# Five reorderings in a forward and backward SSM-convolution / SiLU block on one core

## The chip, the core and the metric

The kernel runs on one of the eight cores of one Trainium2 chip. A core has five engines that run side by side, each with an instruction queue of its own that it works through strictly in order, and they wait for each other through semaphores. TensorE (PE) multiplies matrices into PSUM, VectorE (DVE) and ScalarE (ACT) do element-wise work and copy PSUM to SBUF, GpSimd (POOL) does small element-wise work and issues DMAs, SyncE (SP) only issues DMAs. PSUM here is eight banks of 128 partitions x 2 KB. The metric is the device time of one execution in microseconds (us).

## The reference

Four residual layers run on a [2048, 448] activation, and then the gradient of all of it is taken:

```python
x = A_q
x = x + A(layernorm(x), k, v, shift_k, ssm_k, ssm_D)   # layer 0: long convolution, gated
x = x + B(layernorm(x), w1, w2)                        # layer 1: silu(x w1) w2
x = x + A(layernorm(x), k, v, shift_k, ssm_k, ssm_D)   # layer 2
x = x + B(layernorm(x), w1, w2)                        # layer 3

A: kv = (four-tap causal shift of k with shift_k) * v
   y  = irfft(rfft(kv, 4096) * rfft(ssm_k, 4096))[:2048] + kv * ssm_D
   return q * y
```

It returns x and the gradients of A_q, A_k, A_v, shift_k, ssm_k, ssm_D, w1 and w2 for a given grad_out. k, v and the filter are the same in layers 0 and 2, so y is computed once. All data is bf16, sums are float32.

## The kernel before

Rows are laid out so that partition p holds rows 16p to 16p + 15; a chunk c is four of these 16 row tiles. The kernel has three stages.

**Prefix** (`_ssm_prefix`, to about 102 us) computes y (`Ysb`) by FFTs written as matmuls. A first stage multiplies by `M1sb` (`_fft_stage1`, L206, and `stage1_kv`, L399, for kv), 128 x 128 blocks are turned on PE (`turn`, L361, seven groups of 16), and a second stage multiplies by `Gsb` (`_fft_stage2`, L217, in 14 chunks of 1024 columns, `NCI` = 14). ssm_k is transformed first. Then the shift convolution (`conv`, L383) runs over two halves h of the channels and four row groups; in the second half two of the 14 chunks of the filter's second stage (`Ka`) follow each conv, that is eight of them, and the other six follow the loop. `_swap_halves_dma` (L244, L245) makes from `Ka` a copy `KB` with the two partition halves exchanged, by two DMAs on POOL's queue for each pair of chunks. Also in this loop the layernorm of the first four row tiles runs step by step (`ln0`, `_ln_steps`: statistics on DVE, rstd by a power on POOL, L270, normalised rows `na0` on ACT, L276). After the loop kv is turned and gets its second stage; `cons_prod` copies each chunk (`A1K`), multiplies it on DVE with `Ka` and `KB` (`pab`, L467), and `_fft_inv_stage2_chunk` (L226, L227) does the first inverse stage into the PSUM tile `ps_v`, copied to `B1` (`A1kv`), two chunks later. At the end 16 turns of a part of grad_out (`ps_t`, copied to `gT0`, L485) and eight matmul groups (`ps_y`, L492) give `Ysb`, copied by DVE (the first) and ACT (the other seven). All PSUM tiles of the prefix rotate through four buffers of two banks (tag `A`).

**Main** (`Main.run`) goes over the four chunks c. `H` multiplies by w1 (`ps_h`, L509) and applies silu, `O` by w2 (`ps_o`, L691) and adds to the residual `X` (L695), `G` is the gradient through w2 (`ps_g`, L509; its result is copied on ACT, L719, or multiplied by the silu slope on DVE, L861), `N` the gradient through w1 and the layernorm (`ps_n`, L737). `T` turns four row tiles on PE (`ps_t`, L576) and copies them on ACT (L577). Letters in `weave` and `steps` say in which order steps of these generators are traced; PE's queue keeps this order, the other engines' queues are set by a scheduler that works from the traced order. `fwd0(c)` and `fwd0b(c)` are the first norm with the gate and the second norm of a chunk (L278 on DVE is the normalised result). `ps_o` and `ps_n` share two PSUM banks (tag `po`). `store` (L562, L566, L568) sends every activation tile through a DMA transpose on SP's queue and writes it to DRAM (`a_d`, `g_d`).

**Jobs and suffix.** The weight gradients are products over all 2048 rows. `Jobs` cuts them into blocks of four matmuls (`J` in the patterns; `ps_d`, L1023 in `opening`, L988 in `mms`) that are woven into the last chunk of `Main` and into `_ssm_suffix`, which computes the gradients of the convolution. A job reads one of the stored tiles again as its stationary side (`dstat`, 512 KB, loaded in `load`: the fourth to sixth on POOL's queue, L977, the others on SP's, L982) against one of four moving tensors of 1792 KB: grad_out (`go`), the gradient in `X`, and the normalised rows n3 (`n3m`, loaded by `load_n3`, L1083) and n1 (`n1m`, L1076). `n3m` takes the SBUF of `w2T`, `n1m` that of `go`.

`issue_after(i)` places an instruction behind instruction i in the same queue. It is an order and no wait for i's end.

Of the kernel before, what the change touches and what calls it, by code (L numbers as in the profile page):

```python
# [10 lines left out]
FP32 = mybir.dt.float32  # L11
# [6 lines left out]
P = 128  # L18
S = 2048
D = 448  # L20
F = 1792
J = 16
# [8 lines left out]
NCI = SPEC // 1024  # L31
# [186 lines left out]
        consume(ci, ps)  # L218


def _fft_inv_stage2_chunk(k, pa, pb, conj, B1, ci, psum, cnd=False):
    nc = k.nc
    ga, gb = (G_IAC, G_IBC) if conj else (G_IA, G_IB)
    pv = psum.tile([P, 8, P], FP32, name="ps_v", **k.pt["v"])
    for i in range(8):
        nc.tensor.matmul(pv[:, i, :], lhsT=pa[:, i * P:(i + 1) * P], rhs=k.Gsb[:, ga, :], start=True, stop=False)  # L226
        nc.tensor.matmul(pv[:, i, :], lhsT=pb[:, i * P:(i + 1) * P], rhs=k.Gsb[:, gb, :], start=False, stop=True)  # L227
    if cnd:
        _copy(nc, k.bal.pick(1024), B1[:, :, 32 * ci:32 * ci + 32].rearrange("p q (dh ds) -> p dh q ds", ds=4),
              pv[:].rearrange("p dh (q ds) -> p dh q ds", ds=4))  # L230
    else:
        _copy(nc, k.bal.pick(1024), B1[:, 8 * ci:8 * ci + 8, :].rearrange("p a b -> p (a b)"), pv[:].rearrange("p a b -> p (a b)"))
# [56 lines left out]
def _ssm_prefix(k):  # L289
    nc, tc = k.nc, k.tc  # L290
# [3 lines left out]
    with ExitStack() as es:  # L294
# [110 lines left out]
        def cons_ka(ci, ps):  # L405
            sl = slice(ci * 1024, (ci + 1) * 1024)
            _copy(nc, bal.pick(1024), Ka[:, sl], ps[:])
            if ci % 2 == 1:
                lo, hi = (ci - 1) * 1024, (ci + 1) * 1024
                if ci > 8:  # L410
                    _swap_halves_dma(k, KB, Ka, lo, hi, nc.gpsimd)

        k.gb0 = _hd(k, [P, 4, D], "gb0")
        with tc.issue_after(w2.ins):
# [5 lines left out]
        for h in range(2):  # L420
            for i, jq in enumerate((1, 2, 3, 0)):
                kvt = conv(h, jq)
                if prev:
                    stage1_kv(*prev)
                prev = (h, jq, kvt)
                if h == 0:
                    for g in (2 * i, 2 * i + 1):
                        if g < 7:
                            turn(A1Kf, Z, g)
                else:  # L430
                    _fft_stage2(k, Z, psum, cons_ka, range(2 * i, 2 * i + 2))
                    next(ln0, None)
        for _ in ln0:
            pass
        for i in range(4):
            _swap_halves_dma(k, KB, Ka, 2048 * i, 2048 * (i + 1), nc.gpsimd)
        stage1_kv(*prev)
        _fft_stage2(k, Z, psum, cons_ka, range(8, NCI))

        for i in range(7):  # L440
            nc.gpsimd.dma_start(out=k.SPEC_d["K"][:, 2048 * i:2048 * (i + 1)], in_=Ka[:, 2048 * i:2048 * (i + 1)])
# [34 lines left out]
        k.X = k.wk.tile([P, NT, D], BF16, name="X", tag="WX")  # L476
        k.gT0 = k.X[:].rearrange("p t d -> p (t d)")[:, 11 * D:11 * D + 2048].rearrange("p (b t) -> p b t", b=ND)
        for pa, pb, cj in hold:
            _fft_inv_stage2_chunk(k, pa, pb, False, B1, cj, psum)
        pt = psum.tile([P, ND, 512], BF16, name="ps_t", tag="A", bufs=4)  # L480
        for b, (lo, hi) in enumerate(BLK):
            for tl in range(4):
                nc.tensor.transpose(pt[:, b, tl * P:(tl + 1) * P], k.gb0[:, tl, lo:hi], k.ident[:])
        _copy(nc, bal.pick(2048, dve_ns=0.53), k.gT0, pt[:])

        B1v = B1.rearrange("p a (c n s) -> p a c n s", c=2, n=16)
        for i in range(8):
            py = psum.tile([P, 2, 512], FP32, name="ps_y", tag="A", bufs=4)
            for u in range(2):
                n2 = 2 * i + u  # L490
                for c in range(2):
                    nc.tensor.matmul(py[:, u, :D].rearrange("p (dh ds) -> p dh ds", ds=4), lhsT=k.Minvsb[:, n2, c, :], rhs=B1v[:, :, c, n2, :], start=(c == 0), stop=(c == 1))  # L492
            _copy(nc, nc.vector if i == 0 else nc.scalar, k.Ysb[:, 2 * i:2 * i + 2, :], py[:, :, :D])

# [37 lines left out]
class Main:  # L534
# [21 lines left out]
    def store(self, key, tile_, c, hh):  # L556
        nc, k = self.nc, self.k
        dst = k.OP_d[key]
        prev = None
        for lo, hi in ((0, 4), (4, 7)):  # L560
            an = self.t([P, 4, 4, P], "turned", "S", 2)
            i = nc.sync.dma_start_transpose(out=an[:, 0:hi - lo].rearrange("p a t f -> p (a t) f"), in_=tile_[:, lo:hi, :].rearrange("p a s -> p (a s)"))  # L562
            args = dict(out=dst[:, 7 * hh + lo:7 * hh + hi, 4 * c:4 * c + 4, :], in_=an[:, 0:hi - lo])
            if prev is not None:
                with self.tc.issue_after(i.ins):
                    nc.sync.dma_start(**prev)  # L566
            prev = args
        nc.sync.dma_start(**prev)  # L568

    def transp(self, src, dst, h):  # L570
        nc, k = self.nc, self.k
# [208 lines left out]
    def run(self, es):  # L780
# [52 lines left out]
        for c in range(4):  # L833

            aT2, dT2 = r
            self.slope(dT2)
            if c < 3:
                self.fwd0(c + 1)
            nT = self.nT() if c < 3 else None
            o = self.O(c, 1, aT2)  # L840
            steps("OOOO", O=o)
            if c < 3:
                self.fwd0b(c + 1)
            if c == 0:
                weave("O" * 4, O=o)
            else:
                if c == 1:
                    gh2, g = gh21, g21
                else:
                    gh2 = []  # L850
                    g = self.G(gT, gh2)
                if c == 1:
                    weave("OGGOGGOTOT", O=o, G=g, T=self.T(self.n0[c + 1][1], nT))
                elif c < 3:
                    weave("OGOGGOGGGGTOT", O=o, G=g, T=self.T(self.n0[c + 1][1], nT))
                else:
                    jobs.start()
                    weave("OGOGGOGGGGO", O=o, G=g)
            for lo, hi in ((0, 4), (4, 7), (7, 8), (8, 12), (12, 13), (13, 14)):
                g = gh2[lo // 7][:, lo % 7:lo % 7 + hi - lo, :]  # L860
                nc.vector.tensor_tensor(out=g, in0=self.dpart(dT2, lo, hi), in1=g, op=ALU.mult)  # L861
            if c < 3:
                for hh in range(2):
                    self.store(("g", 1), gh2[hh], c, hh)
            gbc = gb
            n = self.N(c, 1, gh2, lambda tl: gbc[:, tl, :], self.n1[1], self.n1[0])
            G2 = self.X[:, 4 * c:4 * c + 4, :]
            gT = self.nT()
            gh1, dT0 = [], dT1
            tg = self.T(G2, gT)  # L870
            if c < 3:
                r = []
                if c == 0:
                    weave("NTNTNHNNHHNNHHNHH", N=n, T=self.T(self.n0[1][1], nT), H=self.H(c + 1, 0, nT, r, (10, 11)))
                else:
                    weave("NHNNHHNNHHNNHHN", N=n, H=self.H(c + 1, 0, nT, r))
                gb = gb_load(c + 1)
                aT, dT1 = r
                weave("OOOOOOTOTO", O=self.O(c + 1, 0, aT), T=tg)
                self.fwd1(c + 1, [self.chain] * 4)  # L880
                g = self.G(gT, gh1, dT0)
                if c:
                    gT = self.nT()
                    self.load_gT(c + 1, gT)
                    weave("G" * 7, G=g)
                else:
                    weave("G" * 7, G=g)
                self.slope(dT1, self.last_copy)
            else:
                weave("NJNJNJNJNJNJNJN", N=n, J=jg)  # L890
                for hh in range(2):
                    self.store(("g", 1), gh2[hh], c, hh)
                weave("J" * 14 + "TJTJJ", T=tg, J=jg)
                weave("GGGJJGGJJGGJJ", G=self.G(gT, gh1, dT0, (1, 3, 5)), J=jg)
            for hh in range(2):
                self.store(("g", 0), gh1[hh], c, hh)
            n = self.N(c, 0, gh1, lambda tl: self.X[:, 4 * c + tl, :], self.n0[c][1], self.n0[c][0])
            if c < 3:
                r = []
                nT = self.nT()  # L900
                weave("NNTNTNHNNHHNNHHHH", N=n, T=self.T(self.n1[1], nT), H=self.H(c + 1, 1, nT, r, (10, 11)))
            else:
                weave("NJNNJNNJNNJN", N=n, J=jg)
# [14 lines left out]
class Jobs:  # L918
# [48 lines left out]
    def load(self, key, ft):  # L967
# [8 lines left out]
        if i in (3, 4, 5):  # L976
            nc.gpsimd.dma_start(out=st[:], in_=src[:, ft, :, :])  # L977
            return st
        with ExitStack() as es:
            if self.last_ld is not None:  # L980
                es.enter_context(k.tc.issue_after(self.last_ld.ins))
            self.last_ld = nc.sync.dma_start(out=st[:], in_=src[:, ft, :, :])  # L982
# [15 lines left out]
    def group(self, fts, keys, movs, fin, tags=None):  # L998
        ps = {}
        tags = tags or [None] * len(fts)  # L1000
        for i, ft in enumerate(fts):
            st = self.load(keys[0], ft)
            if fts == (5, 6) and i == 1:
                self.load_n3()
            ps[ft] = self.bank(tags[i])
            yield from self.mms(ps[ft], st, movs[0](), 0, NT, True, False)
        if fts == (12, 13):
            self.go2()
        for ft in fts:
            st = self.load(keys[1], ft)  # L1010
            yield from self.mms(ps[ft], st, movs[1](), 0, NT, False, True)
            fin(ft, ps[ft])

# [362 lines left out]
```

## Time and profile before

| | |
|---|---|
| median of 3 timed runs | 720.8 us (720.35 to 721.57) |
| profiled execution | 718.15 us |
| its span, first to last instruction | 716.4 us |
| granted TensorE clock, mean | 1.000 |
| PE / DVE / ACT / POOL busy | 685.9 / 487.7 / 442.2 / 122.9 us |
| DMA | 172.59 MB, mean 241 GB/s |
| prefix, up to the last copy into `Ysb` | about 102 us |
| `Main` with the opening jobs | about 102 to 502 us |
| suffix with the rest of the jobs | about 502 to 716 us |

All positions below are microseconds from the start of the span of the profiled execution. In a timeline line the columns are start, length, engine, source line, operation, output<-input, shapes, the count of merged instructions, and in brackets how long the engine had idled before it and what ended that. An engine name with a q (SPq, ACTq) is its queue issuing a DMA. In the list of waits the columns are total us, number of waits, longest wait. Instructions of one engine overlap a little at their ends, so the distance between two starts is shorter than the length shown.

### The profile page before, as it was taken

The page shows a single profiled execution, that of the slowest core. Times are in us where ns is not written, and L with a number is a line of the kernel's source. Part 1 is how long each engine was busy: PE and PEld are TensorE (multiplying, and loading weights), DVE is VectorE, ACT ScalarE, POOL GpSimd, SP SyncE. Part 2 cuts the span into 40 slices and gives each one's busy share as a digit, 9 for nine tenths or more (in the row PEclk, how much of TensorE's full clock was granted, in tenths as well). Part 3 has the DMA queues.
Part 4 walks back from the last instruction along what each step waited for, and adds up shares of the span by engine and source line. Part 5 has one row for each costly group of instructions (what it writes and reads, how often), then busy time and mean ns, then how long its engine had stood idle before and what let it go on. Part 6 is the DMA issues. An engine that isn't in the chain of part 4 may idle for free.

```text
span 716.4 us, 12787 instructions
## 1 busy us (share of the span) xinstructions
PE 685.9 (96%) x5008; PEld 378.4 (53%) x5008; DVE 487.7 (68%) x1107; ACT 442.2 (62%) x580; POOL 122.9 (17%) x208
## 2 busy tenths in 40 slices
PE   5998889998999999999999999999999999999998
PEld 4886644434444444444444444544466666656655
DVE  3789976668887748876379633925158768869790
ACT  3879877686877968679687784132845555545200
POOL 1024420201011100201001100001212223353130
PEclk9999999999999999999999999999999999999999
DMA  9939999769969999499875998189998887889962
GB/s 289 311 124 243 347 313 230 185 169 264 215 147 242 220 242 245 104 224 274 205 177 134 232 244 323 31 185 271 304 401 313 294 339 248 268 287 363 351 192 86
DMA packets 196237, 172.59 MB, mean 241 GB/s; under 512 B 143090, under 2 KB 174194, under 8 KB 195024
## 3 DMA queue, kind: packets, MB, share of 16 engines
q1 hardware_dynamic: 181280, 115.30, 61.9%
q0 software_dynamic: 13344, 52.54, 20.9%
q10 hardware_dynamic: 1552, 3.94, 1.4%
q8 instruction: 39, 0.64, 0.4%
q14 instruction: 22, 0.18, 0.1%
HBM read 73.25 MB, written 60.10 MB: 186 GB/s over the span
## 4 chain that ended last, share of the span: by engine, by line
PE 75%; ACT 3%; DVE 3%; issue 3%; POOL 1%; DMA 1%; POOLq 0%
PE ps_d L988 20%; PE ps_n L737 12%; PE ps_h L509 11%; PE ps_g L509 11%; PE ps_o L691 8%; PE ps_d L1023 2%; PE ps_v L227 2%; PE ps_v L226 2%; PE ps_t L576 1%; PE ps_gK L1298 1%; PE ps_tr L1204 1%; POOL rstd L270 1%; PE ps_d L1058 1%; PE ps_gkv L1278 1%; PE ps_s L1221 1%
## 5 line engine op out<-in xcount | busy, mean ns | idle before, releaser
L988 PEld LDWEIGHTS <-dstat 128*128 128x128 bf16 x768 | 72.4, 98 | 64.0 <-DMA dstat<-a_d 3.1
L509 PE MATMUL ps_h<-nT,w1sb 128*128 128x512 bf16 (+1 forms) x448 | 97.4, 380 | 2.6 <-ACT dT L674 1.9
L737 PE MATMUL ps_n<-w1T,ghT 128*128 128x448 bf16 x448 | 92.1, 352 | 2.1 <-DVE X L695 2.1
L691 PE MATMUL ps_o<-w2sb,aT 128*128 128x448 bf16 x448 | 88.5, 352 | 0.0
L509 PE MATMUL ps_g<-nT,w2T 128*128 128x512 bf16 (+1 forms) x392 | 82.8, 380 | 0.1
L719 ACT CAST ghT<-ps_g 128x512 bf16<-128x512 f32 (+1 forms) x74 | 54.2, 761 | 41.9 <-PE ps_g L509 41.6
L669 ACT ACTIVATE aT<-ps_h 128x512 bf16<-128x512 f32 (+1 forms) x82 | 60.0, 760 | 29.2 <-PE ps_h L509 27.6
L509 PEld LDWEIGHTS <-w1sb 128*128 128x128 bf16 (+1 forms) x448 | 35.5, 97 | 59.8 <-issue 25.4
L737 PEld LDWEIGHTS <-ghT 128*128 128x128 bf16 x448 | 43.3, 98 | 43.1 <-issue 2.3
L691 PEld LDWEIGHTS <-aT 128*128 128x128 bf16 x448 | 43.5, 98 | 40.1
L509 PEld LDWEIGHTS <-w2T 128*128 128x128 bf16 (+1 forms) x448 | 35.4, 97 | 54.2 <-issue 19.8
L910 DVE SCALAR_TENSOR_TENSOR lb_v<-lb_u,n 128x448 bf16<-128x448 bf16 x48 | 30.0, 624 | 47.1 <-ACT lb_u L741 46.5
L270 POOL TENSOR_TENSOR rstd<-ln_ve,mhalf 128x2 f32<-128x2 f32 (+2 forms) x27 | 22.9, 849 | 198.6 <-DVE ln_ve L268 198.6
L684 ACT ACTIVATE dT<-dT 128x1024 bf16<-128x1024 bf16 (+1 forms) x64 | 55.0, 938 | 0.1
L988 PE MATMUL ps_d<-n1m,dstat 128*128 128x448 bf16 x224 | 48.6, 352 | 0.0
L988 PE MATMUL ps_d<-n3m,dstat 128*128 128x448 bf16 x224 | 48.6, 352 | 0.0
L674 ACT CAST dT<-ps_h 128x1024 bf16<-128x1024 f32 (+1 forms) x50 | 42.9, 874 | 0.0
L741 ACT ACTIVATE lb_u<-ps_n,rstd 128x448 bf16<-128x448 f32 x32 | 20.8, 649 | 33.2 <-PE ps_n L737 25.1
L988 PE MATMUL ps_d<-X,dstat 128*128 128x448 bf16 x160 | 34.2, 353 | 2.7 <-DMA dstat<-a_d 2.7
L577 ACT COPY nT<-ps_t 128x1024 bf16<-128x1024 bf16 x20 | 20.2, 1008 | 22.2 <-PE ps_t L576 22.2
L988 PE MATMUL ps_d<-go,dstat 128*128 128x448 bf16 x160 | 33.7, 353 | 0.0
L861 DVE TENSOR_TENSOR ghT<-dT,ghT 128x512 bf16<-128x512 bf16 (+2 forms) x24 | 18.1, 777 | 19.2 <-ACT ghT L719 19.0
(214 smaller groups left out, 1236.9 us busy)
## 6 DMA issues: line engine op xcount, KB each, us to landing
dstat<-g_d SPq DMA_DIRECT2D x28, 512.0 KB, 5.6
dstat<-a_d SPq DMA_DIRECT2D x23, 512.0 KB, 6.2
a_d<-turned SPq DMA_DIRECT2D x16, 512.0 KB, 4.1
g_d<-turned SPq DMA_DIRECT2D x16, 512.0 KB, 3.9
a_d<-turned SPq DMA_DIRECT2D x16, 384.0 KB, 3.5
g_d<-turned SPq DMA_DIRECT2D x16, 384.0 KB, 3.3
N_d<-n POOLq DMA_DIRECT2D x10, 448.0 KB, 4.6
spec_K<-ZK POOLq DMA_DIRECT2D x7, 512.0 KB, 7.4
```

The source lines that it names most:

```text
L270: k.ln_pow = nc.gpsimd.tensor_tensor(out=r[:, lo:hi], in0=ve[:, 0:n], in1=k.mhalf[:, 0:n], op=ALU.pow)
L509: nc.tensor.matmul(ps(u, u + 1)[:, 0, :], lhsT=wT[h, b, ft * P:(ft + 1) * P], rhs=rhs[h, b, :], start=start, stop=stop)
L577: self.last_copy = nc.scalar.copy(dst[:, 2 * h:2 * h + 2, :], pt[:])
L669: self.last_silu = nc.scalar.activation(aT[hh][:, o:o + hi - lo, :], ps(lo, hi), ACT.Silu)
L674: nc.scalar.copy(self.dpart(dT, 2 * fp + lo, 2 * fp + hi), ps(lo, hi))
L684: self.nc.scalar.activation(d[:, o:o + n, :], d[:, o:o + n, :], ACT.Derivative_silu)
L691: nc.tensor.matmul(po[:, :D], lhsT=aT[ft // 7][:, ft % 7, tl * P:(tl + 1) * P], rhs=self.w2sb[:, ft, :], start=(ft == 0), stop=(ft == NF - 1))
L719: nc.scalar.copy(g, ps(lo, hi))
L737: nc.tensor.matmul(pn[:, :D], lhsT=gh[ft // 7][:, ft % 7, tl * P:(tl + 1) * P], rhs=self.w1T[:, ft, :], start=(ft == 0), stop=(ft == NF - 1))
L741: nc.scalar.activation(u0[:], pn[:, :D], ACT.Identity, scale=k.rstd[2 * L + 1][:, t:t + 1], accum_out=cp[:, tl, 0:1])
L910: nc.vector.scalar_tensor_tensor(out=v[:], in0=u0, scalar=-1.0 / D, in1=n_t, op0=ALU.mult, op1=ALU.mult, accum_out=cp[:, 1:2])
L988: self.nc.tensor.matmul(ps[:, :D], lhsT=st[:, t, :], rhs=mov[:, t, :], start=(first and t == 0), stop=(last and t == NT - 1))
```

## The change

Five edits, none of which changes a result or the number of matmuls:

1. *k's second stage beside the conv*: the four rounds of the second half of the conv loop take 4, 4, 3 and 3 chunks of the filter's second stage instead of 2 each, and none are left behind the loop. All seven pairs of half-swaps are traced after the loop, before the last `stage1_kv`.
2. *Last inverse chunk in two tiles*: the fourteenth chunk of the first inverse stage is computed in two PSUM tiles of four blocks; the first is copied by ACT, the second by DVE. The copy to `gT0` is pinned to DVE, and all eight copies into `Ysb` are on ACT.
3. *A norm behind residual sums*: `fwd0b(1)` is traced after all of `O` of chunk 0, layer 3, instead of halfway.
4. *A turn moved up*: in the last chunk the two steps of the turn `T` come after 11 and 13 jobs instead of after 14 and 15.
5. *A norm's rows loaded behind a job load*: in the job group of feature tiles 5 and 6, which loads four `dstat` tiles (loads number 4 to 7, counted from 0), the load of n3 was traced right after load 5 and is now traced right after load 6; and load 6 is placed behind the last store of `Main` in SP's queue.

```diff
-def _fft_inv_stage2_chunk(k, pa, pb, conj, B1, ci, psum, cnd=False):
+def _fft_inv_stage2_chunk(k, pa, pb, conj, B1, ci, psum, cnd=False, halves=False):
     nc = k.nc
     ga, gb = (G_IAC, G_IBC) if conj else (G_IA, G_IB)
+    if halves:
+        for h, eng in enumerate((nc.scalar, nc.vector)):
+            pv = psum.tile([P, 8, P], FP32, name="ps_v", **k.pt["v"])
+            for i in range(4):
+                c = slice((4 * h + i) * P, (4 * h + i + 1) * P)
+                nc.tensor.matmul(pv[:, i, :], lhsT=pa[:, c], rhs=k.Gsb[:, ga, :], start=True, stop=False)
+                nc.tensor.matmul(pv[:, i, :], lhsT=pb[:, c], rhs=k.Gsb[:, gb, :], start=False, stop=True)
+            _copy(nc, eng, B1[:, 8 * ci + 4 * h:8 * ci + 4 * h + 4, :], pv[:, 0:4, :])
+        return
...
         def cons_ka(ci, ps):
             sl = slice(ci * 1024, (ci + 1) * 1024)
             _copy(nc, bal.pick(1024), Ka[:, sl], ps[:])
-            if ci % 2 == 1:
-                lo, hi = (ci - 1) * 1024, (ci + 1) * 1024
-                if ci > 8:
-                    _swap_halves_dma(k, KB, Ka, lo, hi, nc.gpsimd)
...
                 else:
-                    _fft_stage2(k, Z, psum, cons_ka, range(2 * i, 2 * i + 2))
+                    _fft_stage2(k, Z, psum, cons_ka, range((0, 4, 8, 11)[i], (4, 8, 11, 14)[i]))
                     next(ln0, None)
         for _ in ln0:
             pass
-        for i in range(4):
+        for i in range(7):
             _swap_halves_dma(k, KB, Ka, 2048 * i, 2048 * (i + 1), nc.gpsimd)
         stage1_kv(*prev)
-        _fft_stage2(k, Z, psum, cons_ka, range(8, NCI))
...
-            _fft_inv_stage2_chunk(k, pa, pb, False, B1, cj, psum)
+            _fft_inv_stage2_chunk(k, pa, pb, False, B1, cj, psum, halves=cj == NCI - 1)
...
-        _copy(nc, bal.pick(2048, dve_ns=0.53), k.gT0, pt[:])
+        nc.vector.tensor_copy(k.gT0, pt[:])
...
-            _copy(nc, nc.vector if i == 0 else nc.scalar, k.Ysb[:, 2 * i:2 * i + 2, :], py[:, :, :D])
+            _copy(nc, nc.scalar, k.Ysb[:, 2 * i:2 * i + 2, :], py[:, :, :D])
...
-        nc.sync.dma_start(**prev)
+        self.last_store = nc.sync.dma_start(**prev)
...
             steps("OOOO", O=o)
-            if c < 3:
+            if c in (1, 2):
                 self.fwd0b(c + 1)
             if c == 0:
                 weave("O" * 4, O=o)
+                self.fwd0b(1)
...
-                weave("J" * 14 + "TJTJJ", T=tg, J=jg)
+                weave("J" * 11 + "TJJTJJJJ", T=tg, J=jg)
...
         with ExitStack() as es:
+            if i == 6:
+                es.enter_context(k.tc.issue_after(self.main.last_store.ins))
             if self.last_ld is not None:
                 es.enter_context(k.tc.issue_after(self.last_ld.ins))
             self.last_ld = nc.sync.dma_start(out=st[:], in_=src[:, ft, :, :])
...
         for i, ft in enumerate(fts):
             st = self.load(keys[0], ft)
-            if fts == (5, 6) and i == 1:
-                self.load_n3()
             ps[ft] = self.bank(tags[i])
             yield from self.mms(ps[ft], st, movs[0](), 0, NT, True, False)
...
         for ft in fts:
             st = self.load(keys[1], ft)
+            if fts == (5, 6) and ft == 5:
+                self.load_n3()
             yield from self.mms(ps[ft], st, movs[1](), 0, NT, False, True)
             fin(ft, ps[ft])
```

## The prediction, made before the changed kernel was run

> **What bounds the kernel now.** I read the page first, then the list of what TensorE (PE) waited for, then the timelines of the engines around each of those waits.
>
> ```profile
> PE 685.9 (96%) x5008; PEld 378.4 (53%) x5008; DVE 487.7 (68%) x1107; ACT 442.2 (62%) x580; POOL 122.9 (17%) x208
> ```
>
> PE is busy for 685.9 of 716.4 us at a granted clock of 1.000, so what can be won is the 30.5 us in which it waits. No matmul is removed, so each edit is worth the PE wait that it takes away, less the one it brings.
>
> ```profile
> PE ps_v L226 <- DVE pab L467: 5.3, 6, 1.6
> PE ps_d L988 <- DMA dstat<-a_d: 2.7, 1, 2.7
> PE ps_n L737 <- DVE X L695: 2.1, 1, 2.1
> ...
> PE ps_t L576 <- ACT nT L577: 1.1, 3, 0.4
> ...
> PE ps_d L1023 <- ACT dout L1091: 0.8, 1, 0.8
> ...
> PE ps_y L492 <- DVE A1kv L112: 0.5, 1, 0.5
> ```
>
> Here the reader sees a place for each edit: 2.7 us for the loads, 2.1 for the norm, 0.34 of the 1.1 and 0.78 for the turn (the two waits between 469 and 472 us), 0.5 for the last inverse chunk, and 5.3 (first 1.6 at 70.78) for the inverse chunks that follow k's second stage.
>
> **Loads (n3's rows).** SyncE's queue around the 2.7 us wait, which ends at 520.90:
>
> ```profile
> 488.24 4.47 SPq L562 DMA_TRANSPOSE turned<-ghT  x2
> ...
> 495.57 0.39 SPq L1083 DMA_DIRECT2D n3m<-N_d  x1
> 496.47 13.76 SPq L562 DMA_TRANSPOSE turned<-ghT  x2
> 511.69 0.36 SPq L566 DMA_DIRECT2D g_d<-turned  x1
> 515.63 0.36 SPq L568 DMA_DIRECT2D g_d<-turned  x1
> 516.03 1.10 SPq L982 DMA_DIRECT2D dstat<-a_d  x2
> ...
> 518.28 0.74 SPq L1076 DMA_DIRECT2D n1m<-N_d  x1
> ```
>
> The 1792 KB load of n3 is issued just ahead of the last two transposes. These then hold the queue 13.76 us where the pair before held it 4.47; the first landed 15.2 us after its issue. The tile that PE waits for (call it L6) is queued behind them and takes 4.83 us to land. In the new order the queue runs transposes, stores, L6, n3, then the tile after it (L7); that L6 is tied to the last store adds no wait, only this order. The second transpose needs the store of 495.04 landed (501.1), lands about 4 us later, and the last store goes out near 505.4. L6 must also wait for its buffer: PE ends with the tile in it (the X half of feature tile 4) at 507.88 + 0.76 = 508.6. So L6 goes at about 508.7 and lands near 513.7; PE wants it at 518.25. The whole 2.65 us goes.
>
> What is late next: L7, n1, and a tile that POOL loads. L7 stands behind n3: 509.2 + 11.8 (n3's own time before) = 521.0, and half a megabyte more is 2 us; PE wants it at 527.41 - 2.65 = 524.8. n3 itself is first read at 534.0 - 2.65. n1 is issued at 518.28 as before, because its buffer is read until 517.7, and PE wants it at 537.9 - 2.65 = 535.25. Before it landed at 533.3: L6, L7, two g_d tiles and n1 (3.93 MB) took 17.3 us from 516.03, 228 GB/s. Afterwards, from 508.7, the queue carries L6, n3 and L7 (2.88 MB), of which 2.05 MB are through by 517.7 at that rate; the remaining 0.83 and the 2.88 MB of the two tiles and n1 need 16.3 us: 534.0. Just in time. The POOL tile landed 5.19 us after 505.64 and is wanted at 513.55; a POOL store that ran beside n3 took 8.95 instead of 4.46 us, and 4.5 us more would make PE wait 1.8. Bounds: -2.9 (the 0.24 wait that follows goes too) to 0 (all of it comes back later). I take -2.65, the row itself.
>
> **Rule and row.** The trace shows a load on one queue holding back what is issued after it (15.2 us against 4.8 for the same transpose). [...]
>
> **Norm behind the residual sums.** DVE ahead of the 2.1 us wait, which ends at 169.05:
>
> ```profile
> 165.27 0.95 DVE L861 TENSOR_TENSOR ghT<-dT,ghT 128x1536 bf16<-128x1536 bf16 x1
> 167.16 1.32 DVE L278 TENSOR_SCALAR n<-X,ln_mv,rstd 128x448 bf16<-128x448 bf16 x4 [0.93 <-POOL rstd L270]
> 168.39 0.61 DVE L695 TENSOR_TENSOR X<-X,ps_o 128x448 bf16<-128x448 bf16 x1
> ```
>
> The sum at 168.39 frees the PSUM bank that the first gradient product needs. Of the whole edit the built order changes one thing on DVE: this sum comes ahead of the four normalisations, so it fills the 0.93 gap (166.2 to 166.75). On POOL the rstd power and the store of n keep their places, so they cost nothing new. PE ends its products at 166.97 and starts at once, 2.08 earlier. Next late are the turns of n (ready 168.48, against 168.3) and then the products of ghT (four feature tiles at once): moved up by the sum's 0.53, the large one ends at 170.0 where PE would want it at 169.2, and the last at 171.15. So PE finishes the first gradient tile at 171.34, not 172.15: -0.8. The bounds are -0.5 (DVE's move alone) and -2.08.
>
> **Turn moved up.** PE at the end of the opening jobs (each job 0.76 us):
>
> ```profile
> 469.34 0.61 PE L576 MATMUL ps_t<-ident,X 128*128 128x128 bf16 x8 [0.34 <-ACT nT L577]
> ...
> 471.48 0.92 PE L1023 MATMUL ps_d<-X,dstat 128*128 128x448 bf16 x4 [0.78 <-ACT dout L1091]
> ```
>
> With 11 instead of 14 jobs ahead, the turn starts at 457.04 + 11 x 0.757 = 465.37; its rows X are ready at 465.18, so it just doesn't wait. Two jobs (1.5 us) cover ACT's copy (1.01), and the 0.34 goes. The last job still waits for a copy of the job before (same PSUM tile): 0.2 + 0.54 + 0.05 = 0.8 after that job's end, where today ACT's second turn copy makes it 0.94. The products start at 471.6, not 472.24: -0.6; bounds -0.3 and -1.1.
>
> **Last inverse chunk in two tiles.** Today DVE copies all of it (93.24 to 94.47) and PE starts the last stage at 94.61. Halved, ACT's part (0.53, from ghT's 128x512 rows) runs while PE computes the second half, and DVE's ends 0.69 after it, inside the 16 turns of grad_out (1.06): PE starts as the turns end, -0.5. The first output copy goes from DVE to ACT: eight at 0.82 instead of seven. It starts 0.5 earlier, so the gate on DVE follows by 0.5. The extra PSUM tile shifts the four rotating buffers by one; the first products of the next stage then reuse the fifth and sixth output buffer, free before they are needed. Bounds -0.9 to 0.
>
> **k's second stage beside the conv.** ACT and DVE after the conv:
>
> ```profile
> 60.50 1.93 ACT L111 CAST ZK<-ps_s 128x1024 bf16<-128x1024 f32 x2 [0.20 <-PE ps_s L217]
> 62.31 2.72 ACT L276 ACTIVATE na<-x0c,ln_nmr,rstd 128x448 bf16<-128x448 bf16 x4
> 64.93 3.62 ACT L111 COPY A1K<-ps_tr 128x2048 bf16<-128x2048 bf16 x2
> 68.43 2.86 ACT L111 CAST A1K<-ps_s 128x1024 bf16<-128x1024 f32 x3
> ...
> 69.49 3.50 DVE L467 TENSOR_TENSOR pab<-A1K,ZK 128x2048 bf16<-128x2048 bf16 x3 [1.00 <-ACT A1K L111]
> ```
>
> The products pab begin when ACT has copied the first kv chunk (68.43 + 1.03). The edit moves six of fourteen k chunks (two matmuls, 0.43 us, and a copy of 0.92 on ACT or 1.14 on DVE each) into the conv loop. But there DVE has no room: a round is 1.01 + 0.53 + 1.14 + 0.65 + 0.2 = 3.53 us, which is the loop's pace. Two chunks more make a round 4.7, one of them 1.14 on DVE; DVE then carries 15.5 us from 44.68 to the copy of chunk 11 (60.2), which through the four PSUM buffers lets PE begin kv's turns at 60.7, against 60.82. Nothing is won there. And the built order on ACT is new: the turn copies come first (groups 2 and 4: ready 63.6 and 65.4, ending 65.4 and 67.2), then the four normalisations (2.62, to 69.85), and only then the kv chunk. ACT idles from 61.7 to 63.6, where it does the normalisations now. So pab begins at 70.9 instead of 69.49: +1.4. Through the fourteen products, with the copies on DVE (four as before, the first one a chunk later), 0.3 of the waits there fall away: +1.1. On POOL's queue six of k's fourteen half-swaps (0.52 us each) stand ahead of the rstd power and are out by 60.7, the power comes at 64.7, once DVE has the variance; four or five swaps are behind the store of the normalised rows (69.9) and out by 73, wanted from 83. Bounds: -0.9 (DVE is through with the turns at 68.6, so pab can't start earlier) to +2.
>
> **Sum.** -2.65 - 0.8 - 0.6 - 0.5 + 1.1 = -3.45. Between these places PE waits only on ACT and DVE work that it fed itself, so the shifts pass through. Against the profiled execution (718.15 us, span 716.4 and 1.75 around it) that is 714.7. The three timed runs lie higher (median 720.8), so on their scale it is 717.3.
>
> **Rivals.** (1) k's stage gains what its name says: if ACT isn't the last to arrive, pab starts at 68.6 and the sum is -5.4: 715.4. For it: ACT has 5 us idle in that stretch. Against: its order is fixed. (2) The load's stall only moves: the POOL tile or n1 is late by 1.8 to 2.6, leaving -0.8 to -1.7: 719.1 to 720. For it: 8.95 us for a small store beside n3; against: that store ran beside transposes too. [...]
>
> **Chances.** Forecast 0.62, (1) 0.13, (2) 0.17, (3) 0.08. 0.2% (1.44 us) is about what a measurement of this kernel can tell. The forecast and (1) are faster, nearly all; (2) half. Faster 0.77, same 0.15, slower 0.08. The forecast's own range, with k's stage at +2 or 0, is 716 to 718.5; the range of 715 to 720.4 takes in (1) and (2) and leaves (3) out.
>
> **What will show it.** The wait of PE for dstat gone and the last two transposes at 4 to 5 us each; no wait on X at 169 but about 0.9 on ghT; one wait left of the two near 470; PE's last inverse stage without a wait for DVE; ACT's normalisations of x after the two turn copies and the first pab near 70.9. It is wrong if pab starts before 69.5, or if PE waits for dstat or n1m between 513 and 545.

## The result, and the profile after

The changed kernel takes 716.1 us (median of six runs, 714.2 to 717.6), the kernel before beside it 722.0; the ratio is 0.991 with a 95% interval of 0.988 to 0.994. The forecast was 717.3, in 715 to 720.4. So the time came out as predicted, but in part by luck, through two wrong sizes of opposite sign: the place of n3's load was worth two to three times its price, and moving k's second stage cost about two to three times its own. Ratios, here and below, leave out the seven runs that took over 1.5% longer than the fastest run of the same kernel on the same chip; medians are over all runs.

The profiled execution took 716.31 us with a span of 714.5. From its page, each engine's busy time and the granted clock in 40 slices:

```profile
PE 689.3 (96%) x5008; PEld 380.9 (53%) x5008; DVE 486.2 (68%) x1106; ACT 444.2 (62%) x582; POOL 123.3 (17%) x208
PEclk9999899999999999999999999999999999999999
```

PE is busy 3.4 us longer than before with the same 5008 matmuls, and the fifth slice (71 to 89 us) no longer runs at full clock. From the list of waits after, what PE waited for (total us, number, longest):

```profile
PE ps_v L235 <- DVE pab L471: 7.4, 5, 3.6
...
PE ps_n L741 <- DVE ghT L866: 0.8, 1, 0.8
PE ps_t L580 <- ACT nT L581: 0.7, 2, 0.4
...
PE ps_d L1030 <- ACT dout L1098: 0.6, 1, 0.6
...
PE ps_g L513 <- ACT Ysb L111: 0.5, 1, 0.5
```

Gone are the 2.7 us on dstat, the 2.1 on X and the 0.5 ahead of the last inverse stage. The wait on pab grew from 5.3 to 7.4, its longest from 1.6 to 3.6, and a wait of the first gradient product on a copy into Ysb is new.

Two executions don't begin alike: PE waits 5.6 us for one of the first loads (`ZK`) before and 4.9 after, and the first matmul of the conv is at 27.27 us before and at 26.19 after. Below, positions in the prefix are therefore counted from that matmul, written "c + ...". The first matmul of H is at c + 79.97 before and at c + 83.03 after: the two edits of the prefix together lost 3.06 us. From H on, the changed kernel wins back 0.72 us up to the end of the first gradient products, another 0.64 up to the products behind the turn, and 2.70 where PE waited for dstat.

The loss arises around the first products pab. VectorE's timeline there, after (in brackets the time the engine had stood idle, and what ended it):

```profile
64.45 2.36 DVE L112 COPY A1K<-ps_tr 128x2048 bf16<-128x2048 bf16 x2 [0.22 <-PE ps_tr L370]
68.97 2.36 DVE L471 TENSOR_TENSOR pab<-A1K,ZK 128x2048 bf16<-128x2048 bf16 x2 [2.16 <-ACT A1K L111]
72.98 2.43 DVE L471 TENSOR_TENSOR pab<-A1K,ZK 128x2048 bf16<-128x2048 bf16 x2 [1.66 <-DMA ZK<-ZK]
77.12 1.23 DVE L112 CAST A1K<-ps_s 128x1024 bf16<-128x1024 f32 x1 [1.70 <-PE ps_s L217]
```

ScalarE's timeline of the same stretch:

```profile
61.77 3.65 ACT L111 COPY A1K<-ps_tr 128x2048 bf16<-128x2048 bf16 x2 [1.70 <-PE ps_tr L370]
65.32 2.72 ACT L285 ACTIVATE na<-x0c,ln_nmr,rstd 128x448 bf16<-128x448 bf16 x4
67.94 2.81 ACT L111 CAST A1K<-ps_s 128x1024 bf16<-128x1024 f32 x3
```

And TensorE's first inverse product:

```profile
70.25 0.29 PE L235 MATMUL ps_v<-Gsb,pab 128*128 128x128 bf16 x1 [3.65 <-DVE pab L471]
```

Three things are seen. ACT's order is the predicted one: two turn copies, four normalisations, and only then the first kv chunk, and VectorE waits 2.16 us for it. (A half-swap of k that the first product also waits for, issued at 58.20, landed at 68.83, only 0.14 us before that product began.) The third product pab then waits 1.66 for a half-swap of k, which the prediction did not have. And TensorE, idle for 3.65 us, comes back at half speed. The busy times by stretch, after, show that last point (first the stretch and its length, then the busy times of PE, PEld, DVE, ACT and POOL with their instructions, then the granted clock, the DMA share and GB/s):

```profile
62.00:69.00 7.00, 4.60 (x66) 3.64 (x63) 4.58 (x7) 7.00 (x8) 3.27 (x6) 1.00 1.04 257
69.00:76.00 7.00, 5.75 (x44) 4.65 (x45) 4.76 (x4) 4.94 (x6) 3.39 (x7) 0.51 1.04 274
76.00:83.00 7.00, 5.88 (x83) 4.67 (x81) 5.85 (x6) 5.65 (x7) 3.51 (x8) 1.00 1.03 305
```

The drop lasts from 69.02 to 75.85, 6.83 us, in which matmuls of 128 columns start 0.107 us apart instead of 0.056.

SyncE's queue around the loads, after:

```profile
497.39 6.39 SPq L566 DMA_TRANSPOSE turned<-ghT  x2
505.52 0.36 SPq L570 DMA_DIRECT2D g_d<-turned  x1
506.68 0.36 SPq L572 DMA_DIRECT2D g_d<-turned  x1
507.08 0.56 SPq L989 DMA_DIRECT2D dstat<-a_d  x1
507.81 0.33 SPq L1090 DMA_DIRECT2D n3m<-N_d  x1
```

The last two transposes hold the queue for 6.39 us instead of 13.76, and the tile PE had waited for is issued at 507.08.

### The profile page after: what moved, and what is told of

It is laid out like the page before. It is cut to its first block, busy times and chain, and to the rows that moved or that the text cites. A ratio compares the mean times of both kernels' runs of the same rounds, so it can differ in the third digit from the quotient of the medians.

```text
span 714.5 us, 12786 instructions
## 1 busy us (share of the span) xinstructions
PE 689.3 (96%) x5008; PEld 380.9 (53%) x5008; DVE 486.2 (68%) x1106; ACT 444.2 (62%) x582; POOL 123.3 (17%) x208
## 4 chain that ended last, share of the span: by engine, by line
PE 62%; issue 8%; DVE 5%; ACT 4%; DMA 3%; POOL 2%; POOLq 0%; DVEq 0%; ACTq 0%
PE ps_d L995 12%; PE ps_n L741 12%; PE ps_h L513 11%; PE ps_g L513 10%; PE ps_o L695 7%; PE ps_d L1030 3%; ACT dT L688 2%; DMA ksf<-KS_d 1%; PE ps_t L580 1%; PE ps_gK L1305 1%; PE ps_tr L1211 1%; POOL rstd L279 1%; PE ps_d L1065 1%; PE ps_s L206 1%; DVE n L287 1%
```

## The experiments

All twelve were timed in turn with the kernel before, in three groups, each on a chip of its own (e1 to e4, e5 to e9, e10 to e13). The ratio is to the kernel before on the same chip. The columns "first pab" and "H" are positions of the profiled run counted from the first matmul of the conv; "half clock" is the length of the stretch at 0.5 near 70 us.

| run | what it is | median us (runs) | ratio [95%] | first pab | H | half clock |
|---|---|---|---|---|---|---|
| before | | 722.0 (6) | 1 | 42.22 | 79.97 | 0 |
| after | | 716.1 (6) | 0.991 [0.988, 0.994] | 42.78 | 83.03 | 6.83 |
| e5 | after, again | 714.7 (6) | 0.990 [0.987, 0.993] | 42.77 | 82.26 | 3.41 |
| e1 | after, k's stage back | 713.1 (5) | 0.984 [0.980, 0.987] | 42.21 | 80.25 | 3.41 |
| e13 | e1 again | 712.7 (6) | 0.989 [0.985, 0.992] | 42.22 | 79.43 | 0 |
| e12 | e13, last inverse chunk back too | 714.5 (12) | 0.991 [0.987, 0.994] | 42.22 | 79.97 | 0 |
| e2 | before, k's stage moved alone | 728.4 (12) | 1.006 [1.004, 1.009] | 42.84 | 84.24 | 6.83 |
| e10 | after, load of n3 back | 724.6 (12) | 1.003 [0.998, 1.007] | 42.77 | 82.98 | 6.83 |
| e3 | after, PE kept busy (also in the suffix) | 719.0 (6) | 0.992 [0.990, 0.995] | 42.77 | 82.13 | 0 |
| e6 | after, PE kept busy | 714.8 (6) | 0.990 [0.986, 0.993] | 42.77 | 82.00 | 0 |
| e4 | after, half-swaps on SyncE | 717.5 (6) | 0.990 [0.986, 0.993] | 42.77 | 83.05 | 6.83 |
| e7 | e6 and e4 together | 712.5 (6) | 0.986 [0.982, 0.989] | 42.77 | 80.45 | 0 |
| e9 | e4, normalisations behind kv copies | 712.6 (6) | 0.987 [0.984, 0.991] | 40.63 | 80.45 | 0 |
| e11 | e1, PE kept busy | 713.1 (6) | 0.989 [0.986, 0.993] | 42.21 | 79.92 | 0 |

**The changed kernel again,** unedited.

> The changed kernel itself once more, unedited, as the measure for the three runs beside it on the same chip: the first measurement gave 0.991 of the kernel before, 714.2 to 717.6.

714.7 us, ratio 0.990: the first measurement is confirmed. Its half clock lasted 3.41 us instead of 6.83, and H came 0.77 earlier.

**k's second stage back where it was.** In the changed kernel:

```diff
-            range((0, 4, 8, 11)[i], (4, 8, 11, 14)[i])
+            range(2 * i, 2 * i + 2)
...
+        # four pairs of half-swaps behind the loop, the other three in cons_ka, as before
+        _fft_stage2(k, Z, psum, cons_ka, range(8, NCI))
```

> The changed kernel with k's second stage back where it was: two chunks in each of the four conv rounds, six behind the loop, the half-swaps placed as before; the other four edits stay. Theory 1 (the move of k's stage costs time): in the profile of the changed kernel the first gradient-independent stage H starts 2.0 us later than before although the start of the run was 1.1 us earlier, so the prefix lost about 3 us; most of it should come back: 2 to 3 us faster than the changed kernel (716.1), 713 to 714, ratio to before 0.987 to 0.988, with the TensorE clock at 1.0 around 70 us. Theory 2 (the price on record, +1.1 from ACT's order alone): 715.0, ratio 0.990. Rival (the last inverse chunk in two tiles is what lost the time): within 0.5 us of the changed kernel.

> e1_k_back once more, unedited, as the measure for the two runs beside it: 712.1 to 715.0 in its first call, 0.984 of the kernel before.

Over both measurements the eleven runs have a median of 713.1, the twelve runs of the changed kernel one of 715.3: the move costs about 2 us, though these runs weren't made on the same chip. By position, which tells more, it costs 2.8 (e5 to e13) to 3.6 (after to e13). Theory 1 holds, the price on record (+1.1) is too low. e1 had a half-clock stretch of 3.41 us after waits of 0.51 and 1.59; e13 had none after 0.50 and 1.59. Up to the first product their positions agree to 0.01; their H lies 0.82 apart. What decided between them these runs don't show.

**k's second stage moved alone**, in the kernel before (the reverse of the edit above).

> The kernel before with only k's second stage moved beside the conv. Theory 1 (the move costs 2 to 3 us through the late first product, the half clock and the late half-swap): ratio to before 1.003 to 1.004, a stretch at half clock near 70 us, the first product pab about 0.5 later than in the kernel before. Theory 2 (price on record): +1.1 us, ratio 1.0015. Rival (the move gains what it is named for): ratio below 0.999.

It is slower, as theory 1 says, but by 0.6%, some 4.5 us, more than foretold. The prefix lost 4.27 us by position, of which 1.30 is a wait of the first gradient product for the last copy into Ysb; and in its profile the wait for dstat has grown from 2.65 to 6.24 us, with another 6.83 us at half clock from 525.09, near the end of that wait:

```profile
PE ps_d L983 <- DMA dstat<-a_d: 6.2, 1, 6.2
```

This wait is followed up below.

**TensorE kept busy in its wait for the first product.**

```diff
     pv = psum.tile([P, 8, P], FP32, name="ps_v", **k.pt["v"])
+    for _ in range(48 if ci == 0 and not cnd else 0):      # second version: "not conj"
+        nc.tensor.matmul(pv[:, 0, :], lhsT=k.Gsb[:, ga, :], rhs=k.Gsb[:, gb, :], start=True, stop=True)
     for i in range(8):
```

> The changed kernel with 48 extra 128x128 matmuls (2.7 us at full clock) of constants into the PSUM tile of the first inverse chunk, ahead of its own products, which then overwrite them: TensorE is busy in the 3.65 us in which it waited for the first product. Theory (an idle TensorE is what brings the half clock at 69.0 us): no stretch at 0.5, clock 1.000 in every run. The two chunks behind the first product then take 1.3 instead of 2.5 us each, but the third product waits for its half-swap until 72.98 as before, so the third chunk starts at 74.3 instead of 75.34: 1 to 1.5 us faster than the changed kernel, 714.6 to 715.1, and the times lie closer together (716.31, 714.17, 717.26, 714.75, 717.55, 715.86 in the changed kernel). Rival 1 (the half clock comes from something else, as the 1.0 clock after longer waits elsewhere could mean): still 0.5 there, time the same. Rival 2 (the half clock is hidden by the late half-swap): clock 1.0, time the same within 0.4.

> The changed kernel with the 48 extra matmuls in the prefix alone. In e3_pe_busy the helper that holds them is also called in the suffix, so 48 more (2.7 us) ran there and its total can't be compared. Counted from the start of the conv, e3_pe_busy reached H 0.9 us earlier than the changed kernel and showed a wait of 1.6 us ahead of the third inverse chunk. Theory (half clock and late half-swap lie side by side, each hides most of the other): clock 1.000, H 0.9 us earlier, 0.5 to 1 us faster than the unedited kernel in this call. Rival (the half clock is worth all that separates the runs at clock 1.000 from those at 0.995 in the changed kernel, 714.5 against 717.0): 2 us faster.

The first version's total says nothing: the helper also runs in the suffix, where the extra matmuls took 2.7 us. In both, the half clock near 70 us is gone (granted clock 1.00 from 62 to 83 us in e6, 0.51 from 69 to 76 in the changed kernel), so an idle TensorE is what brings it. H comes 0.90 and 1.03 earlier than in the first profile of the changed kernel, and 0.26 (e6) earlier than in e5. In the times nothing can be told apart (714.8 against 714.7). What takes the place of the slow stretch is seen in VectorE's timeline of the second version:

```profile
68.81 2.36 DVE L473 TENSOR_TENSOR pab<-A1K,ZK 128x2048 bf16<-128x2048 bf16 x2 [2.16 <-ACT A1K L111]
73.13 2.36 DVE L473 TENSOR_TENSOR pab<-A1K,ZK 128x2048 bf16<-128x2048 bf16 x2 [1.96 <-DMA ZK<-ZK]
```

The wait for the half-swap is still there, and now TensorE waits behind it (1.49 us ahead of the third inverse chunk, where the changed kernel had none).

**Half-swaps issued by SyncE, ahead of the loads of w1.**

```diff
-            _swap_halves_dma(k, KB, Ka, 2048 * i, 2048 * (i + 1), nc.gpsimd)
+            _swap_halves_dma(k, KB, Ka, 2048 * i, 2048 * (i + 1), nc.sync)
```

> The changed kernel with the fourteen half-swaps of k issued by SyncE, ahead of the three loads of w1 in its queue, instead of by GpSimd. Theory (the loads of w1, issued at 57.7 to 58.9, make the half-swaps land 9 to 13 us after their issue, and the third product waits 1.66 us for one of them): the half-swaps land before 69, VectorE no longer waits for one at 73. But the TensorE work behind it runs at half clock until 75.8 without a gap, so what is gained is hidden: within 0.5 us of the changed kernel, 715.6 to 716.1, unless the earlier rstd power (GpSimd no longer has half-swaps ahead of it) lets ACT begin the normalisations earlier, which gives at most 0.5 more. Rival (the half-swap is what bounds this stretch): 1.7 us faster, 714.4.

VectorE's three first products follow each other without a wait, and H doesn't move: c + 83.05 against 83.03. The half-swaps did not land before 69 as expected; the second pair landed at c + 43.4 and c + 44.4 instead of c + 44.7 and c + 46.6, just early enough. So the wait of 1.66 us is real and costs nothing as long as the half clock lies over it.

**Both together** (the two diffs above).

> Both at once: the 48 extra matmuls in the prefix and the half-swaps on SyncE ahead of the loads of w1. Theory (two covers over the same 2 us): the wait of 1.6 ahead of the third inverse chunk goes too, H starts 2 to 2.5 us earlier than in the changed kernel counted from the start of the conv (0.9 of it from the clock, nothing from the half-swaps alone as e4_swaps_sp showed, the rest only together). 2 to 2.5 us faster than the unedited kernel. Rival (something else, the pace of VectorE and ACT, takes the place of the half-swap): not more than 1 us.

VectorE's timeline:

```profile
68.64 3.50 DVE L473 TENSOR_TENSOR pab<-A1K,ZK 128x2048 bf16<-128x2048 bf16 x3 [2.15 <-ACT A1K L111]
73.04 1.23 DVE L473 TENSOR_TENSOR pab<-A1K,ZK 128x2048 bf16<-128x2048 bf16 x1 [0.90 <-ACT A1K L111]
```

H is at c + 80.45: 2.58 earlier than in the first profile, 1.81 earlier than in e5, and 1.55 earlier than with the busy TensorE alone. The time is 2.2 us under e5 on the same chip. The theory of two covers holds: 0 from one, 0.3 to 1.0 from the other, 1.8 to 2.6 from both.

**The normalisations behind the kv copies, half-swaps on SyncE.**

```diff
+                with k.tc.issue_after(k.kv_copy.ins):        # the third kv chunk's copy
                     nc.scalar.activation(n_g[:, tl, :], src(tl), ACT.Identity, ...)
...
-        for _ in ln0:
-            pass
...
+            if ci == 3:                                      # in cons_prod
+                for _ in ln0:
+                    pass
```

> The changed kernel with the half-swaps on SyncE, and with ACT's four normalisations of x placed behind the third kv chunk's copy in its order instead of ahead of the first. Theory (ACT's order is what makes the first product late, as the prediction says): the first product pab starts when VectorE is through with its turn copies, 2.2 us earlier counted from the start of the conv (40.6 instead of 42.8), TensorE waits 1.5 instead of 3.65 us for it and stays at clock 1.0 or drops for one stretch of 3.4 us at most; the third product doesn't wait; H 2.5 to 3.5 us earlier, and the time 2.5 to 3.5 us under the unedited kernel. Rival (VectorE's pace over fourteen products sets the end, whenever the first starts): the first product earlier, H less than 1 us earlier.

The first product starts at c + 40.63, 2.14 earlier, and TensorE waits 1.50 us for it: ACT's order does make it late, to the tenth. But H gains only 1.8 against e5, because the third product comes to the half-swap earlier and waits longer for it, as VectorE's timeline shows:

```profile
65.97 2.36 DVE L472 TENSOR_TENSOR pab<-A1K,ZK 128x2048 bf16<-128x2048 bf16 x2
71.43 2.36 DVE L472 TENSOR_TENSOR pab<-A1K,ZK 128x2048 bf16<-128x2048 bf16 x2 [3.10 <-DMA ZK<-ZK]
```

This half-swap landed at 71.31, 10.8 us after its issue. The time is 2.1 us under e5, less than the 2.5 to 3.5 expected.

**The load of n3 back.**

```diff
             st = self.load(keys[0], ft)
+            if fts == (5, 6) and i == 1:
+                self.load_n3()
...
-            if fts == (5, 6) and ft == 5:
-                self.load_n3()
...
-            if i == 6:
-                es.enter_context(k.tc.issue_after(self.main.last_store.ins))
```

> The changed kernel with the load of n3 back behind load 5, ahead of the last two transposes in SyncE's queue; the tie of load 6 to the last store is gone too. [...] Rival (the gain at this place is no more than the 2.65 of one profile): 2.6 slower, 717.4 to 718.7.

724.6 us, 1.2 to 1.3% above the two measurements of the changed kernel as ratios, that is 8 to 9 us: more than the wait for dstat in the two profiles that had it with n3's load at this place, 2.65 us before and 6.24 in e2. From its list of waits:

```profile
PE ps_d L993 <- DMA dstat<-a_d: 9.2, 2, 7.1
```

SyncE's queue ahead of this wait:

```profile
497.47 0.40 SPq L1088 DMA_DIRECT2D n3m<-N_d  x1
499.56 18.84 SPq L566 DMA_TRANSPOSE turned<-ghT  x2
...
523.00 1.48 SPq L987 DMA_DIRECT2D dstat<-a_d  x2
```

TensorE at the ends of the two waits:

```profile
518.72 1.68 PE L993 MATMUL ps_d<-go,dstat 128*128 128x448 bf16 x4 [7.10 <-DMA dstat<-a_d]
...
527.96 0.93 PE L993 MATMUL ps_d<-X,dstat 128*128 128x448 bf16 x4 [2.14 <-DMA dstat<-a_d]
```

The two transposes hold the queue 18.84 us here (13.76 in the profile before, 6.39 after). The dstat tile that GpSimd loads, issued at 503.55 while they hold it, landed at 518.67, 15.1 us later instead of the 5.2 of the profile before, and it is this tile that TensorE waits 7.10 us for. Then four matmuls take 1.68 us instead of 0.92, since the clock is at half for 6.83 us from 516.77, and the tile behind the transposes still comes 2.14 late. For most of the 15.1 us n3's rows were not in flight: n3 had landed at 506.83, and the second transpose was issued only then. For the next 10 us two transposes and GpSimd's loads are in flight without n3 (129 and 205 GB/s between 505 and 518 us). Why they take so long together is open; that the edit (n3's place and the tie of load 6, undone here together) removes it is shown. The profile of the kernel before, with its one wait of 2.65 and a clock of 1.000, was a mild execution. Of the 48 runs of it that the ratios of e1 to e13 use, four had a clock of 1.000 and took 714.3 to 717.8 us; the other 44, at 0.991 to 0.998, took 718.8 to 728.8.

**TensorE kept busy, k's stage back** (e1 with 20 extra matmuls in the prefix).

> k's second stage back where it was (as in e1_k_back), and 20 extra matmuls (1.1 us) ahead of the first inverse chunk in the prefix, where TensorE waits 1.6 us. Theory (e1_k_back lost 0.8 us between the first product and the end of the inverse chunks to one half-clock stretch of 3.4 us): clock 1.000 in that part, H 0.3 to 0.8 us earlier than in e1_k_back counted from the start of the conv (79.45 to 79.95 instead of 80.25); 0 to 0.8 us faster than e13_k_back_again, and under the changed kernel by 2.5 to 3.5 us, the fastest of all versions here. Rival: the extra matmuls come in the way of the first product's chunk, same or slower.

H is 0.33 us earlier than in e1, within what was expected, but not earlier than in e13, which had no half clock either, and the time shows no gain. The inverse chunks end 0.20 earlier than in e13, and the first gradient product then waits 0.54 us for a copy into Ysb, which it doesn't in e13.

**The load of n3, the norm and the turn alone.**

```diff
-            _fft_inv_stage2_chunk(k, pa, pb, False, B1, cj, psum, halves=cj == NCI - 1)
+            _fft_inv_stage2_chunk(k, pa, pb, False, B1, cj, psum)
...
+        # k's second stage back as in e1; copy into gT0 by the planner, first copy into Ysb on VectorE
```

> The kernel before with the norm, the turn and the load of n3 changed, without k's second stage and without the last inverse chunk in two tiles. By the prediction's terms 0.5 us slower than e13_k_back_again beside it (the two tiles), by the profiles 0.53 from the last inverse chunk to the first output product (1.41 us in the kernel before, 0.88 in e1_k_back). Rival (the eighth output copy on ACT takes it back at the first gradient product): same time, H at the same place counted from the start of the conv.

H is at c + 79.97, the place of the kernel before to the hundredth, and at c + 79.43 in e13: the two tiles give 0.54 us. The start of the last inverse stage on TensorE in e12:

```profile
93.79 6.23 PE L501 MATMUL ps_y<-A1kv,Minvsb 128*128 128x448 bf16 x32 [0.52 <-DVE A1kv L112]
```

The same in e13, without a wait:

```profile
90.96 6.23 PE L501 MATMUL ps_y<-A1kv,Minvsb 128*128 128x448 bf16 x32
```

The medians differ by 1.8, but the runs of e12 spread from 710.8 to 723.4, so the times say no more than the sign. Against the kernel before, the three edits that are left give 0.9%, 6.8 us.

## Why the prediction was right, and where it was wrong

**The load of n3: right for the profiled wait, size wrong.** Between the two profiled executions the term is what was predicted, 2.70 against 2.65. Its working was rough in detail: the freed tile landed at 517.15 and not at 513.7, with n3 in flight beside it (10.1 us from issue to landing against 4.8 before), 1.7 us before PE wanted it; n3 landed at 521.47 (521.0 predicted), n1 at 533.26 (534.0), L7 at 523.22. So the second rival fell: nothing moved on to GpSimd's tile or n1. Nor was the changed kernel slower, to which 0.08 was given: that n3 ahead of n1 in SyncE's queue makes n1 late no run shows. In after n1 landed 14.2 us after its issue, 15.0 before, and what SyncE issued there moved at 220 GB/s (5.77 MB from 507.08 to 533.26), against 228 before. In e13 PE wants the freed tile 5.5 us earlier than in the changed kernel and it lands only 3.2 earlier; waits of 0.72 and 0.83 for two dstat tiles are left, so the margin is thin.

The step that failed is the one that took "the row itself" as the size and carried 2.65 from the profile to the median as a constant. The wait's length was that of one execution at clock 1.000; undone on the chip the edit is worth 8 to 9 us in the median (e10), and 5.4 by e12 (6.8 less the 1.36 of the norm and the turn). In e10 the longest wait is moreover for GpSimd's tile, which came in time in the profile before, so the row didn't hold all that the load's place does. The gap between the profiled 718.15 and the medians of 720.8 and 722 was a sign: it was itself largely this wait, judging by the clocks of the runs, and the edit takes it away. The runs beside e12 bear this out: among those at clock 1.000 the kernel before takes 715.7 (median of three) and e12 712.7 (of seven), 3.0 us apart, near the 4.0 that the rows give for the load, the norm and the turn, while the ratio, over runs at any clock, gives 6.8. But the timed runs carry no trace, so that last reading is argued from two profiles (e2, e10) and the clocks, not shown run by run.

**The norm: right.** No wait on X, 0.77 on ghT at 172.00 (0.9 predicted), gain 0.72 for 0.8.

**The turn: right.** One wait left, 0.62 for 0.8 predicted; gain 0.64 for 0.6.

**Two tiles: right,** 0.54 for 0.5. The remark that the buffers taken over by the next stage are "free before they are needed" fails in the changed kernel: the first gradient product starts at 102.66, 0.05 after the seventh copy's end. This comes with k's stage moved (0.54 in after, e3 to e7 and e10, 1.30 in e2) and not with the two tiles (none in e1 and e13). But e9 has k's stage moved and no such wait, and e11 has the wait without it. What decides which copy the product must wait for stays open here.

**k's second stage: sign right, size and reasons wrong.** Predicted +1.1 with bounds of -0.9 and +2; measured +2.6 without any half clock (e6 against e13), up to +3.6 with it. By steps:
- "Nothing is won" in the loop: kv's turns begin at c + 32.70 instead of 33.54, so 0.84 is won.
- "pab begins ... +1.4": the order on ACT is as worked out and the first product is later by 0.56 (the 1.4 less that 0.84). With the half-swap and the clock out of the way 0.3 of it is left at the end of the inverse chunks (e7 against e13). In the changed kernel another order on ACT alone would have won no more than 0.14 there, because the half-swap that the first product waits for landed just then; that ACT's order makes the first product 2.1 late is shown by e9 against e4, both with the half-swaps on SyncE. By its letter the sign named, a pab before 69.5, did appear (68.97), only because this execution began 1.08 earlier.
- "four or five swaps ... out by 73, wanted from 83": this step looked at the last pairs and at their issue. The second pair is wanted for the third product, was issued at 58.71 and 59.22, and took 12.2 and 13.5 us to land. Price 1.55 (e7 against e6).
- The granted clock was taken as 1.000 throughout. The wait ahead of the first inverse chunk went from 1.59 to 3.65 us, and that brought the half clock: 0.3 to 1.0 at H, depending on whether 3.41 or 6.83 us of it come.
- From the end of the inverse chunks to H another 0.7, of which 0.54 is the wait on the copy into Ysb. With the 0.3 and the 1.55 this makes the 2.6.

With that the first rival, a gain at this place, fell too: pab could start no earlier than ACT and the first half-swaps let it, and what e9 won there by another order on ACT it lost to the half-swap.

On clocks, the stretches at half speed lasted 3.41 us (e1, e5) or 6.83 us (after, e2, e4, e10, and once more in the suffix of e2 and e10); e12's trace has no record of the clock, its profiled run is listed at 1.000. In the changed kernel the drop came 2.4 us after PE had stopped, within the wait of 3.65 us; the drops in the suffix came within the waits of 6.24 us (e2) and 7.10 us (e10). The wait for the first inverse chunk of 3.6 to 3.7 us went with a drop in after, e2, e4 and e10. The wait of 2.65 us in the profile before had none (clock 1.000). But so long a wait isn't needed: e1 dropped after two waits of 0.51 and 1.59, while e13 and the profile before, with the same waits, did not. The 3.41 us ahead of e1's drop and the 3.41 us of it (columns as above):

```profile
66.60:70.01 3.41, 1.43 (x6) 0.39 (x4) 2.40 (x3) 3.41 (x4) 1.18 (x3) 1.00 1.06 223
70.01:73.42 3.41, 3.30 (x26) 2.76 (x27) 2.32 (x3) 1.94 (x3) 1.03 (x2) 0.50 1.01 315
```

PE is idle for 1.98 us of the first stretch. In a stretch of the same length in the profile before that holds both waits, 67.37 to 70.78, it is idle for 2.09 (busy 1.32), and the clock stays at 1.00. So neither the waits nor this idle time tells e1 from the other two; what does, these runs don't show.

**The sum.** On the profile's scale 714.7 was predicted and 716.31 came: the prefix lost 3.06 us where the sum had 0.6, the other three edits gave 4.06 where it had 4.05, and a start 1.08 earlier, which is chance, gave part of it back; 0.2 more was lost in the suffix. On the scale of the medians the undersized load pulled the other way by 3 to 6 us, and the kernel before stood at 722 rather than 720.8. That the two errors nearly cancelled is luck. Taking k's stage back is faster than both kernels (713.1 over eleven runs against 715.3 over twelve of the changed one, on different chips); e7 and e9 at 712.5 are not told apart from it.

## What to carry to other kernels

Price a wait for a transfer from more than one execution: if the runs spread by 1% and the profiled one is at their lower end, the wait in its profile may be a mild one, and removing its cause can be worth two or three times the row. Of a set of transfers that is moved, price the first one wanted by its landing, not the last one by its issue. And where two late things end at the same place, taking one away shows little; e4 gave 0, e6 at most 1.0, and both together up to 2.6. Before one of them is named as the cause, look when the other ended: the first product's half-swap landed 0.14 us before it.

## What the runs showed of the hardware that was not expected

- The last two DMA transposes landed 13.9 and 11.6 us after their issue in e2 and 21.8 and 15.8 in e10, against 8.1 and 4.6 in after. The 1792 KB load was in flight beside the first of each pair alone; it had landed (e10, at 506.83), or was about to, when the second was issued. A 512 KB load on GpSimd's queue took 15.1 us in e10 against 5.2 before and 6.1 after.
- Half-swaps within SBUF (256 KB each, fourteen of them) landed 4 to 14 us after their issue, 9.2 in the median, on GpSimd's queue (after); the one that the third product waits for in e9, on SyncE's queue, landed 10.8 us after its issue.
- The clock of TensorE went to half for 6.83 us in waits of 3.65 (after), 6.24 (e2) and 7.10 us (e10), and stayed at 1.000 with one of 2.65 (before). Two waits of 0.51 and 1.59 us were followed by 3.41 us at half clock in e1, and 0.50 and 1.59 by none in e13.
